# Adding x for two tiles at once with four 64x64 products at the end of an attention and spectral-mixing kernel

## The chip, the cores and the metric

The kernel runs on one core of one Trainium2 chip. The metric is the device time of one execution in microseconds (us). The engines are called PE (TensorE), DVE (VectorE), ACT (ScalarE), POOL (GpSimd) and SP (SyncE, which issues the loads and stores here).

## The reference

Two layers are computed one after the other. The first is attention with a sliding window of 128 and a linear bias per head; the second keeps the 64 lowest modes of a Fourier transform along the sequence, multiplies each mode by a complex 512x512 matrix, transforms back and adds a ReLU branch.

```
scores = scale * q @ k^T ; mask: 0 <= rel < 128 ; bias = -slope[h] * |rel|
attn = softmax(scores) ; x = attn @ v          # [8, 576, 512] after joining 8 heads of 64
X = rfft(x, axis=1)[:, :64]                    # Xr, Xi
Yr = Xr @ w_r - Xi @ w_i ; Yi = Xr @ w_i + Xi @ w_r      # 64 modes, 512x512 each
y = irfft(Y, n=576, axis=1)
u = x + y
return u + max(u @ w_ch, 0)
```

## The kernel before

The work on the attention is done in units of one pair of heads and one batch entry; the result x stays on chip in bf16 as `g.x_sb` (128 rows at a time, four such tiles per batch entry) and `g.x4` (the last 64 rows of two batch entries in one tile). `g.seq` lists the 36 tiles of x in the order in which they are finished: for an even batch entry four tiles, for the odd one behind it four, then their shared tile, so nine for two batch entries.

The weights of the modes, 134 MB, stream through a ring of three buffers per matrix (`_load_w`, line 586), and `_modes` (lines 621 and 625) multiplies one mode at a time. The first group of 128 input rows is done beside the attention, the other 384 rows, the last group, in a stage of its own. In that stage, after some of the modes, one tile of x is taken further: `_xt` transposes it and `_xw` (line 669) multiplies it by w_ch. `_xw` leaves x @ w_ch in SBUF as two bf16 parts, a rounded one and its remainder (`g.hl`, lines 673 and 674). For tiles of way "q" (line 87) x itself is added in the same PSUM tile by one more product (line 667).

When the modes are done, `_finish` runs over the 36 tiles. For each tile i PE issues, through `_pair` (two products of 64 output columns at tile positions (0, 0) and (0, 64), line 656):

- the hl pair into `mm[i]` (x @ w_ch, for way q with x in it), in `_known`;
- for way "a" the x pair into `y[i]`, also in `_known`;
- a pair of inverse transform times ZW into `mm[i]` and a pair of inverse transform times Z into `y[i]`.

`mm` and `y` have three PSUM buffers each (`fps`). For i = 0, 1 and 2 `_known` is issued before the last four modes, for the others in the loop. One turn later the tile is evacuated. Way a: ACT makes r = relu(mm) (line 783), and a turn after that DVE adds y (line 792) and SP stores the tile. Way q: ACT copies y to SBUF (line 786), DVE makes r = max(mm, x) (line 787), a turn later POOL adds the two (line 795), and another turn later SP stores. r and ys have four buffers, o has six. Before the change 18 tiles are of way a and 18 of way q.

The last four modes of all batch entries come late: `_z_late` computes them for four batch entries at once (lines 707 and 713), and `_z_take` copies one batch entry's rows to SBUF three tiles ahead of the first tile that needs them, ZW on ACT (line 723), Z on DVE (727) or ACT (725). All engines follow the order in which the program issues (`manual_schedule`).

Of the kernel before, what the change touches and what calls it, by code (L numbers as in the profile page):

```python
# [9 lines left out]
FP32 = mybir.dt.float32  # L10
# [6 lines left out]
P = 128  # L17
# [17 lines left out]
def kernel(  # L35
# [10 lines left out]
    nc = tc.nc  # L46
# [5 lines left out]
    g = Ctx()  # L52
# [30 lines left out]
    for b in range(B):  # L83
        g.seq += [(g.x_sb[:, b, st], ((b, st * P), (b, st * P + 64))) for st in range(4)]
        if b % 2:
            g.seq.append((g.x4[:, b // 2], ((b - 1, 4 * P), (b, 4 * P))))
    g.way = ["q" if 2 <= i < len(g.seq) - 5 and i % 5 in (0, 2, 3) else "a" for i in range(len(g.seq))]

    with tc.manual_schedule(engines={ET.SP, ET.PE, ET.Activation, ET.DVE, ET.Pool}):
        with ExitStack() as wctx:  # L90
# [4 lines left out]
            with ExitStack() as actx:  # L95
# [63 lines left out]
                for n in range(3, N + 2 + TAIL):  # L159
# [9 lines left out]
                    h = (len(w) + 1) // 2  # L169
# [14 lines left out]
            with ExitStack() as xctx:  # L184
                xt = xctx.enter_context(tc.tile_pool(name="xts", bufs=2))
                xps = xctx.enter_context(
                    tc.tile_pool(name="xps", bufs=2, space=bass.MemoryType.PSUM))
                eps = xctx.enter_context(
                    tc.tile_pool(name="eps", bufs=1, space=bass.MemoryType.PSUM))
                todo, done, k = list(tiles[last]), 0, 0  # L190
                xT = _xt(g, 0, xt, xps)
                while done < NM - 4:
                    m0, mg = todo.pop(0)
                    _modes(g, last, m0, mg, last=True)
                    done = m0 + mg

                    while k < len(g.seq) and k * (NM - 4) < done * len(g.seq):
                        nxt = _xt(g, k + 1, xt, xps) if k + 1 < len(g.seq) else None
                        _xw(g, k, xT, xps)
                        xT, k = nxt, k + 1  # L200
                    if 5 <= done < 9:
                        _ft(g, done - 5, xt, xps)
                    for b in range(B):
                        if m0 <= NM - 14 + b < done:
                            _z_early(g, b, eps)
# [3 lines left out]
            for i in range(3):  # L209
                _known(g, i)  # L210
# [4 lines left out]
            for m0, mg in todo:  # L215
                _modes(g, last, m0, mg, last=True)
                if NM - 4 <= m0 < NM - 1:
                    for i in range(BUSY):
                        nc.tensor.matmul(
                            idle, lhsT=g.ident_b, rhs=g.x_sb[:, i % B, 0], start=True, stop=True)  # L220
# [432 lines left out]
def _pair(nc, out, lhsT, rhs, **kw):  # L653

    for h in range(2):
        nc.tensor.matmul(  # L656
            out[64 * h : 64 * h + 64], lhsT=lhsT[h], rhs=rhs[h], tile_position=(0, 64 * h), **kw)


def _xw(g, n, xT, psum):  # L660


    nc = g.nc
    x = g.seq[n][0]
    xw = psum.tile([P, g.DM], FP32, tag="xw", name="xw")
    if g.way[n] == "q":
        nc.tensor.matmul(xw, lhsT=g.ident_b, rhs=x, start=True, stop=False)
    for dt in range(4):
        nc.tensor.matmul(xw, lhsT=xT[:, dt], rhs=g.wch[:, dt],  # L669
                         start=(dt == 0 and g.way[n] != "q"), stop=(dt == 3))  # L670
    for h in range(2):
        hi, lo = slice(64 * h, 64 * h + 64), slice(64 - 64 * h, 128 - 64 * h)
        nc.scalar.copy(g.hl[hi, n, h], xw[hi])  # L673
        nc.vector.tensor_tensor(  # L674
            out=g.hl[lo, n, h], in0=xw[hi], in1=g.hl[hi, n, h], op=ALU.subtract)


def _z_early(g, b, psum):
# [40 lines left out]
def _z_take(g, b):  # L719
    nc = g.nc  # L720
    zp, zwp = g.late
    ks = slice(32 * (b % 4), 32 * (b % 4) + 32)
    nc.scalar.copy(g.ZW[ks, b], zwp[ks])
    if b % 4 == 2:
        nc.scalar.copy(g.Z[ks, b], zp[ks])
    else:
        nc.vector.tensor_copy(g.Z[ks, b], zp[ks])


def _known(g, i):  # L730

    nc = g.nc
    x = g.seq[i][0]
    g.mm[i] = g.fps.tile([P, g.DM], FP32, tag="mm", name="mm")
    g.y[i] = g.fps.tile([P, g.DM], FP32, tag="y", name="y")
    _pair(nc, g.mm[i], [g.ident2] * 2, [g.hl[:, i, h] for h in range(2)], start=True, stop=False)
    if g.way[i] == "a":
        _pair(nc, g.y[i], [g.ident_b[:, 0:64], g.ident_b[:, 64:128]], [x] * 2,
              start=True, stop=False)


def _finish(g):
# [5 lines left out]
    with ExitStack() as fctx:  # L748
# [4 lines left out]
                 for b in range(g.B)]  # L753
        _z_late(g, 0, lps)
        _z_take(g, 0)
        o, r, y = {}, {}, {}

# [7 lines left out]
        for i in range(N + 3):  # L765
            if i < N:
                if i >= 3:
                    _known(g, i)
                ft = [g.FT[:, b % 4, s : s + 64] for b, s in g.seq[i][1]]
                _pair(nc, g.mm[i], ft, [g.ZW[:, b] for b, _ in g.seq[i][1]],  # L770
                      start=False, stop=True)
                _pair(nc, g.y[i], ft, [g.Z[:, b] for b, _ in g.seq[i][1]],
                      start=(g.way[i] == "q"), stop=True)
            if i == first[3] - 1:
                _z_late(g, 4, lps)
            for b in range(1, g.B):
                if i == first[b] - 3:
                    _z_take(g, b)
# [50 lines left out]
```

## Time and profile before

| what | value |
|---|---|
| median of 3 runs | 463.44 us (461.84 to 464.57) |
| span of the profiled execution, first to last instruction | 460.1 us |
| the profiled execution's own time | not given apart from the span; the median is 3.3 us above the span |
| PE busy | 326.6 us (71%), 5939 matmuls |
| DVE, ACT, POOL busy | 226.3 us (49%), 187.9 us (41%), 149.6 us (33%) |
| DMA | 173.92 MB, 378 GB/s in the mean |
| mean granted TensorE clock | 0.754 |

A busy time counts when any instruction of the engine ran. In lines of groups the columns are line, engine, operation, output and inputs, shapes and count, then busy time, mean duration in ns and idle time before them with what ended it. In the timeline they are start, duration, engine, line, operation and count.

### The profile page before, as it was taken

The page shows a single profiled execution, that of the slowest core. Times are in us where ns is not written, and L with a number is a line of the kernel's source. Part 1 is how long each engine was busy: PE and PEld are TensorE (multiplying, and loading weights), DVE is VectorE, ACT ScalarE, POOL GpSimd, SP SyncE. Part 2 cuts the span into 40 slices and gives each one's busy share as a digit, 9 for nine tenths or more (in the row PEclk, how much of TensorE's full clock was granted, in tenths as well). Part 3 has the DMA queues.
Part 4 walks back from the last instruction along what each step waited for, and adds up shares of the span by engine and source line. Part 5 has one row for each costly group of instructions (what it writes and reads, how often), then busy time and mean ns, then how long its engine had stood idle before and what let it go on. Part 6 is the DMA issues. An engine that isn't in the chain of part 4 may idle for free.

```text
span 460.1 us, 14005 instructions
## 1 busy us (share of the span) xinstructions
PE 326.6 (71%) x5939; PEld 229.5 (50%) x5939; DVE 226.3 (49%) x492; ACT 187.9 (41%) x345; POOL 149.6 (33%) x255
## 2 busy tenths in 40 slices
PE   2778797797868985576646655566566578877994
PEld 2557576676757864343334433333333345534552
DVE  8776588658666572333323233133331334512884
ACT  3986576576664660223212122122221123412883
POOL 7697799677676522000000000000000000000882
PEclk9985689768895796566665577566655759979999
DMA  8999999999999999999999999999999999994697
GB/s 251 309 352 326 343 335 394 389 383 381 387 386 396 388 355 362 418 426 358 422 425 423 421 425 424 422 424 425 424 421 424 424 423 401 421 425 182 234 332 258
DMA packets 68382, 173.92 MB, mean 378 GB/s; under 512 B 5600, under 2 KB 21984, under 8 KB 68320
## 3 DMA queue, kind: packets, MB, share of 16 engines
q1 hardware_dynamic: 67936, 171.99, 96.9%
q0 software_dynamic: 384, 1.05, 0.9%
q8 instruction: 46, 0.75, 0.6%
q14 instruction: 16, 0.13, 0.1%
HBM read 163.58 MB, written 9.44 MB: 376 GB/s over the span
## 4 chain that ended last, share of the span: by engine, by line
DMA 48%; PE 32%; issue 6%; ACT 5%; DVE 3%; POOL 3%; SPq 2%; ACTq 0%; POOLq 0%; DVEq 0%
DMA wi<-in_moe_w_i_dram 42%; PE sc L428 6%; PE acc L625 4%; DMA v<-in_v_dram 4%; PE acc L621 4%; PE tqk L402 4%; PE av L481 3%; PE xt L523 3%; PE xw L669 2%; PE mm L656 2%; ACT qkT L410 1%; PE tp L647 1%; PE y L656 1%; SPq L345 1%; ACT hl L673 1%
## 5 line engine op out<-in xcount | busy, mean ns | idle before, releaser
L673 ACT CAST hl<-xw 64x512 bf16<-64x512 f32 x72 | 41.8, 580 | 165.2 <-PE xw L669 137.4
L625 PEld LDWEIGHTS <-wi 128*128 128x128 bf16 x1024 | 66.1, 104 | 79.6 <-DMA wi<-in_moe_w_i_dram 72.9
L795 POOL TENSOR_TENSOR o<-r,ys 128x512 f32<-128x512 f32 x18 | 22.5, 1277 | 247.1 <-DVE r L787 245.0
L625 PE MATMUL acc<-Xlast,wi 128*128 128x16 bf16 x768 | 56.0, 193 | 53.7 <-DMA wi<-in_moe_w_i_dram 53.7
L440 ACT ACTIVATE att<-sc 128x512 bf16<-128x512 f32 (+1 forms) x128 | 72.4, 592 | 45.2 <-PE sc L428 44.5
L621 PEld LDWEIGHTS <-wr 128*128 128x128 bf16 x1024 | 70.0, 106 | 41.9 <-DMA wr<-in_moe_w_r_dram 24.5
L674 DVE TENSOR_TENSOR hl<-xw,hl 64x512 bf16<-64x512 f32 x72 | 49.6, 689 | 83.2 <-ACT hl L673 83.1
L621 PE MATMUL acc<-Xlast,wr 128*128 128x16 bf16 x768 | 62.8, 194 | 21.7 <-DMA wr<-in_moe_w_r_dram 18.0
L391 POOL CAST vb<-v 64x256 bf16<-64x256 f32 x128 | 65.3, 510 | 28.8 <-PE av L481 19.4
L443 DVE TENSOR_TENSOR att<-att,mask 128x512 bf16<-128x512 bf16 x96 | 50.7, 556 | 31.2 <-ACT att L440 30.9
L428 PE MATMUL sc<-qkT,qkT 64*64 64x256 bf16 (+1 forms) x512 | 54.2, 325 | 12.5 <-ACT att L440 5.1
L669 PE MATMUL xw<-wch,xT 128*128 128x512 bf16 x144 | 60.1, 563 | 0.0
L649 DVE COPY xT<-tp 128x512 bf16<-128x512 bf16 x36 | 15.2, 423 | 58.3 <-PE tp L647 57.9
L410 ACT COPY qkT<-tqk 128x576 bf16<-128x576 bf16 x64 | 41.1, 644 | 4.9 <-PE tqk L402 4.9
L402 PE MATMUL tqk<-ident_b,qkb 64*64 64x64 bf16 x1152 | 33.1, 213 | 13.1 <-POOL qkb L380 8.7
L428 PEld LDWEIGHTS <-qkT 64*64 64x64 bf16 x512 | 31.5, 127 | 20.3 <-issue 11.3
L402 PEld LDWEIGHTS <-qkb 64*64 64x64 bf16 x1152 | 32.4, 129 | 15.4 <-POOL qkb L380 10.4
L481 PE MATMUL av<-vb,att 64*128 64x65 bf16 (+1 forms) x1024 | 31.8, 211 | 3.5 <-issue 3.5
L481 PEld LDWEIGHTS <-att 64*128 64x128 bf16 (+1 forms) x1088 | 26.7, 109 | 9.4 <-issue 5.9
L669 PEld LDWEIGHTS <-xT 128*128 128x128 bf16 x144 | 18.7, 135 | 21.6 <-issue 19.1
L380 POOL CAST qkb<-k 128x576 bf16<-128x576 f32 x32 | 26.1, 816 | 0.3 <-PE tqk L402 0.3
L380 POOL CAST qkb<-q 128x576 bf16<-128x576 f32 x32 | 23.7, 739 | 4.8 <-PE tqk L402 1.6
(107 smaller groups left out, 440.7 us busy)
## 6 DMA issues: line engine op xcount, KB each, us to landing
wr<-in_moe_w_r_dram SPq DMA_DIRECT2D x85, 768.0 KB, 8.3
wi<-in_moe_w_i_dram SPq DMA_DIRECT2D x85, 768.0 KB, 9.7
q<-in_q_dram SPq DMA_DIRECT2D x32, 288.0 KB, 7.2
k<-in_k_dram SPq DMA_DIRECT2D x32, 288.0 KB, 7.3
v<-in_v_dram SPq DMA_DIRECT2D x64, 128.0 KB, 6.5
out_dram<-o SPq DMA_DIRECT2D x32, 256.0 KB, 2.8
vt<-in_v_dram POOLq DMA_DIRECT2D x8, 128.0 KB, 7.2
wchf<-in_moe_w_ch_dram SPq DMA_DIRECT2D x2, 512.0 KB, 7.9
```

The costliest lines, as they stand in the source:

```text
L380: g.nc.gpsimd.tensor_copy(tb, t)
L391: g.nc.gpsimd.tensor_copy(o[64 * hh : 64 * hh + 64, i], u.v[64 * i : 64 * i + 64, hh])
L402: g.nc.tensor.transpose(tp[hs, r, :], u.b[w][hs, r], g.ident_b[hs, hs], tile_position=(64 * hh, 64 * hh))
L428: nc.tensor.matmul(sc[hs, r * nq : (r + 1) * nq], lhsT=kT[hs, kt * P + r : kt * P + P : 2], rhs=qT[hs, kt * P : kt * P + nq], start=True, ...
L440: nc.scalar.activation(a[:, :cols], sc[:, :cols], AF.Exp, scale=1.0 / math.sqrt(g.D))
L443: nc.vector.tensor_tensor(out=a, in0=a, in1=g.mask[:, s], op=ALU.mult)
L481: nc.tensor.matmul(av[o, hh, col(t)], lhsT=a[hs, c0 : c0 + m], rhs=vb[hs, 0 : D + 1], start=(j == 0), stop=(j == len(terms) - 1), tile_pos ...
L621: nc.tensor.matmul(o, lhsT=wr[:, a].bitcast(BF16)[:, 1::2][:, c], rhs=X[:, a, 1:3, :, m], start=(a == 0), stop=False)
L625: nc.tensor.matmul(o, lhsT=wi[:, a].bitcast(BF16)[:, 1::2][:, c], rhs=X[:, a, 0:2, :, m], start=False, stop=(a == A - 1))
L669: nc.tensor.matmul(xw, lhsT=xT[:, dt], rhs=g.wch[:, dt], start=(dt == 0 and g.way[n] != "q"), stop=(dt == 3))
L673: nc.scalar.copy(g.hl[hi, n, h], xw[hi])
L674: nc.vector.tensor_tensor(out=g.hl[lo, n, h], in0=xw[hi], in1=g.hl[hi, n, h], op=ALU.subtract)
```

## The change

The ways are laid out in a pattern of nine: tiles 0, 1, 4 and 5 of nine are of way a, the others q, and the last three tiles are a. That makes 19 tiles of way a and 17 of way q. Tiles 0 and 1, and tiles 4 and 5, of each nine form a twin. For the second tile of a twin `_xw` exchanges the upper and lower 64 rows of x in place: a pair of products with the identity into a buffer of the `xw` tag, and a copy by ACT. In `_known` the first tile of a twin then takes two y buffers and issues four products of 64x64, one in each quadrant of the array, which add x for both tiles; the second tile issues none. In `_z_take` the Z copy of batch entries 3 and 7 moves from DVE to ACT, where those of 2 and 6 already are.

```
-    g.way = ["q" if 2 <= i < len(g.seq) - 5 and i % 5 in (0, 2, 3) else "a" for i in range(len(g.seq))]
+    g.way = ["a" if i % 9 in (0, 1, 4, 5) else "q" for i in range(len(g.seq))]
+    g.way[-3:] = ["a"] * 3
+    g.twin = {i: i + 1 for i in range(len(g.seq) - 3) if i % 9 in (0, 4)}
...
     # _xw, at its end
+    if n in g.twin.values():
+        sw = psum.tile([P, g.DM], FP32, tag="xw", name="sw")
+        _pair(nc, sw, [g.ident_b[:, 64:128], g.ident_b[:, 0:64]], [x] * 2, start=True, stop=True)
+        nc.scalar.copy(x, sw)
...
     # _z_take
-    if b % 4 == 2:
+    if b % 4 >= 2:
         nc.scalar.copy(g.Z[ks, b], zp[ks])
...
     # _known
-    x = g.seq[i][0]
     g.mm[i] = g.fps.tile([P, g.DM], FP32, tag="mm", name="mm")
-    g.y[i] = g.fps.tile([P, g.DM], FP32, tag="y", name="y")
+    if i not in g.y:
+        g.y[i] = g.fps.tile([P, g.DM], FP32, tag="y", name="y")
     _pair(nc, g.mm[i], [g.ident2] * 2, [g.hl[:, i, h] for h in range(2)], start=True, stop=False)
-    if g.way[i] == "a":
+    if i in g.twin:
+        j = g.twin[i]
+        g.y[j] = g.fps.tile([P, g.DM], FP32, tag="y", name="y")
+        for t, up in ((i, 0), (j, 64)):
+            for h in range(2):
+                ks = slice((64 * h + up) % P, (64 * h + up) % P + 64)
+                nc.tensor.matmul(
+                    g.y[t][64 * h : 64 * h + 64], lhsT=g.ident_b[ks, ks], rhs=g.seq[t][0][ks],
+                    start=True, stop=False, tile_position=(ks.start, 64 * h))
+    elif g.way[i] == "a" and i not in g.twin.values():
+        x = g.seq[i][0]
         _pair(nc, g.y[i], [g.ident_b[:, 0:64], g.ident_b[:, 64:128]], [x] * 2,
               start=True, stop=False)
```

## The prediction

> **What bounds the kernel now.** I read the page's slices first, then the end in windows, its groups by form, its waits, and last its timeline on TensorE (PE). Until about 421 us the DMA engines are the limit:
>
> ```profile
> PEclk9985689768895796566665577566655759979999
> DMA  8999999999999999999999999999999999994697
> ```
>
> One digit is 11.5 us: the DMA row is at 9 from slice 2 to slice 36, so work that other engines do beside the weight loads is free as long as it does not hold back the next load. The change adds a little there. The rest of it lies behind 421 us, in `_finish`:
>
> ```profile
> 428.00:432.00 4.00, 3.85 (x36) 2.31 (x34) 3.84 (x7) 3.81 (x8) 3.73 (x4) 1.00 0.80 301
> 436.00:440.00 4.00, 4.00 (x40) 2.18 (x38) 3.59 (x7) 3.63 (x8) 3.87 (x4) 1.00 0.96 338
> 444.00:448.00 4.00, 3.66 (x34) 2.19 (x31) 3.09 (x6) 3.93 (x8) 3.39 (x3) 1.00 0.76 291
> L656 PE MATMUL y<-x_sb,ident_b 128*64 128x512 bf16 x28 | 5.7, 382 | 0.8 <-DVE o L792 0.5 <-ACT ys L786 0.3
> DVE o L792 <- DMA out_dram<-o: 1.9, 3, 0.9
> ```
>
> The columns of a window are its length, then busy time of PE, weight load, DVE, ACT and POOL, granted clock, DMA share and GB/s. PE, DVE, ACT and POOL are all nearly full, so this stage is four balanced engines coupled by three `mm` and three `y` buffers. In the timeline a busy PE starts a pair of 64-column products every 0.215 us:
>
> ```profile
> 432.68 0.41 PE L656 MATMUL mm<-ZW,FT 128*64 128x512 bf16 x2
> 432.90 0.41 PE L656 MATMUL y<-Z,FT 128*64 128x512 bf16 x2
> 433.24 1.09 PE L707 MATMUL zwl<-wch,ZT 128*32 128x512 bf16 x16
> 434.15 0.42 PE L713 MATMUL zl<-ident_b,ZT 128*32 128x128 bf16 x16
> 434.50 0.41 PE L656 MATMUL mm<-hl,ident 128*64 128x512 bf16 x2
> ```
>
> From the first ZW product (423.85) to the last pair (453.74) PE starts 72 mm/y pairs, 33 hl pairs and 16 x pairs (three hl and two x were done before): 121 x 0.215 = 26.0 us, and 1.3 us of `_z_late`. Starts further apart than 0.215 give the waits: 428.66 to 429.23 (0.36 over), 440.17 to 440.80 (0.42), 444.52 to 444.92 (0.19), 446.86 to 447.62 (0.55), 451.57 to 452.45 (0.67), two smaller ones 0.2: 2.4 us. So PE is what sets the end, at 92%, and its waits come from buffers that ACT or DVE free late; the longest is the tail's, where DVE's o waits for a store 0.94 us (451.70).
>
> **Part 1, the x products in `_finish`.** Before: 18 tiles of way a, 16 of their x pairs on the path, 16 x 0.215 = 3.44 us. After: 8 twins and 3 single tiles; the twin (0, 1) is issued before the last modes, so 7 quads and 3 pairs stay. If the four products run at once, the quads stream 7 x 0.215. No row shows four 64x64 quadrants at once. The nearest: two 64x64 products on the diagonal do overlap (8 of 256 columns in 0.40 us, 159.76 to 160.16, where one by one at the 0.107 us that 256 columns take would be 0.85), and four of 32 columns do (16 of 512 in 0.91 us above). The ends are 0.215 and 0.43 per quad; I take 0.215, since these rows show both kinds of division overlapping. But a quad changes the tile size from 128x64 to 64x64 and back. The rows above price that: 432.90 to 433.24 is 0.34, 0.125 over a pair's 0.215; the 16 zl products stream 4 x 0.053 = 0.21 and the next pair comes 0.35 later, 0.14 over. Thus a quad costs 0.215 + 0.125 + 0.14 = 0.48, where two pairs cost 0.43. Sum: 7 x 0.48 + 3 x 0.215 = 4.0, against 3.44: **+0.55 us**. Ends: -1.3 without any price for the switch (7 x 0.215 + 3 x 0.215 = 2.15), +2.05 with quads of 0.43.
>
> The Trainium skill, TensorEngine Tiling (Array Packing), section Key Properties, says that changing the tiling mode, not just the tile, drains TensorE; by its promise in the same section that tiles operate independently alone, x would be 1.3 us cheaper, by the drain rule it is not. The trace agrees with the drain, 0.125 and 0.14 us.
>
> **Part 2, the waits.** A quad writes y of two tiles, so with three y buffers it waits until tile i-2 and i-3 are both evacuated; a single x pair needed only one free buffer. Behind that wait on PE stand the FT pairs of tile i, and behind these ACT, DVE and the stores. Twins start at i%9 = 0 and 4.
> At i%9 = 4 the two buffers are those of the ys copy of tile 2 (of the nine) and of the o add of tile 1, and DVE reaches that add late. With hl of tile 0 at time 0, by the spacings above: quad 0.34, mm0 0.70, y0 0.91, mm1 1.34, mm2 1.99, y2 2.20, hl4 3.06, quad 4 ready at 3.40. ACT starts 0.44 after a pair starts (432.90 to ys at 433.34) and takes 0.6: ys of the tile before 0.22, then ZW of `_z_take` (0.58) about 0.83, r0 1.4 to 2.0. DVE takes 0.69 and starts every 0.61: o0 2.03, then r2 (emitted ahead of o1) 2.64, o1 3.25 to 3.94. So quad 4 starts at 3.99, 0.6 late. Where `_z_take` also puts Z on ACT, which the change does for b = 3 and 7 (twins at 13 and 31), r0, o0 and o1 are 0.49 later (ZW at 427.51, Z at 428.00): 1.1 late. Sum over tiles 4, 13, 22, 31: 0.6 + 1.1 + 0.6 + 1.1 = 3.4 us.
> At i%9 = 0 (9, 18, 27) both are way q, or freed earlier, and the copy of tile i-2 ends 1.1 us after its y pair started, about when the quad is ready: 0.
> Against this all 2.4 us of old waits go: their places (y after a, q by turns) vanish, and in the tail o of tile 31 to 34 reuse buffers of tiles 25 to 28, of which 27 and 28 are now stored straight from DVE and not after POOL (1277 ns). What is late next is r on ACT. **+1.0 us**; ends -1.7 (o1 in time at all four, 0.7 of other waits) and +2.5 (all four 1.1, half of the old waits stay).
>
> **Part 3, DVE, ACT, POOL.** One q tile becomes a: POOL 17 adds, 21.7 us instead of 22.5; DVE 36 adds as before, and six Z copies become four, -1.4; ACT +1.1 (2 x 0.57). By start spacing (0.61, 0.5 to 0.6) DVE stays under 25 and ACT under 27 of some 31 us: none becomes the limit by its sum, and the place where ACT's Z is late is in part 2. Stores: 40 DMAs before and after; those of q tiles still go one turn later than those of a. Nothing.
>
> **Part 4, the exchange in `_xw`.** Eight times a pair (0.215 at full clock, 0.43 at half), two switches and an ACT copy of 0.59, in the stage where PE is busy 23.4 of 40 us and ACT 7.9. The cover is the weight ring, three modes deep, some 3.7 us each. It is thin in two places: DMA was down to 0.80 in 214 to 218 and 0.95 in 386 to 390, just where tiles 5 and 32 are exchanged. Ends 0 and +1.2 (both delays of 0.6 passed on); I take **+0.3**.
>
> **Sum.** 0.55 + 1.0 + 0.3 = 1.85 us on the profiled span of 460.1; the median of the runs, 463.44, is 3.3 above that span, which I leave as it is: 465.2, 0.4% up.
>
> **Rivals.**
> First, slower by more: the four products go two at a time. For it: no row shows four. Then PE streams 7 x 0.215 = 1.5 us more: 466.7. It decides from a quad of about 0.3 us upward. Chance 0.20.
> Second, faster: switches hide in the waits (an engine that waits anyway drains for nothing) and o1 comes in time since DVE has two Z less. Then x is 1.3 cheaper and half of the old waits go, 1.2, with the exchange free: 461.0. Against it: r2 stands ahead of o1 on DVE whatever the load. Chance 0.13.
> Third, it does not do what it says: what PE saves is waited for at the y buffers, so gain and loss cancel, 463.4. For it: four engines above 90% in the same windows. Chance 0.22.
> The forecast itself has 0.45, with an own range of 463.7 to 466.8.
>
> **Numbers.** 0.5%, about what a measurement of this kernel can tell from no change, is 2.3 us: bounds 461.1 and 465.8. Of the forecast's 0.45 a third lies above (0.15), of the first rival 0.17, and 0.03 of the third: slower 0.35. Of the second rival 0.07, and 0.01 of the third lies below: faster 0.08. Same is 0.57. The range runs from 461.6, most of the way to the second rival, to 467.6, over the first one with the upper end of part 2.
>
> **What would show it.** Right: quads whose four products start within some 0.1 us, with gaps of 0.1 to 0.15 before and after; PE idle before the quads of tiles 4, 13, 22, 31, released by DVE o; 0.5 us or more longer from the first ZW product to the last o; the stage before 421 us within 0.5 us of now. Wrong: quads of 0.4 us (first rival); no gap around them, or no wait for o (second); a loss ahead of 421 us above 1 us would break part 4.

## The result and the profile after

The change makes the kernel slower by a little: 464.56 us in the median of 22 runs against 462.78 us of the kernel before in as many; the ratio is 1.0046, with a 95% interval of 1.0025 to 1.0067. That is 2.1 us more (1.2 to 3.1). The forecast was 1.85 us, 0.4%, and the time named, 465.2 us, lies 0.6 us above the one measured. The forecast had started from 463.44 us, the median of three runs; that of 22 is 0.7 us lower. The profiled execution has a span of 463.0 us, 2.9 us above that of before.

The slices of the page, one digit for 11.6 us:

```profile
PEclk9989597978876785556575578556665569958998
DMA  8999999999999999999999999999999999992787
```

The DMA row is full up to the end of the modes as it was; the four slices behind it are the end that the change is about. The same windows as before (length, then busy time of PE, weight load, DVE, ACT, POOL, granted clock, DMA share, GB/s):

```profile
428.00:432.00 4.00, 3.53 (x30) 1.62 (x30) 2.78 (x6) 3.02 (x6) 2.51 (x2) 1.00 0.61 228
436.00:440.00 4.00, 4.00 (x58) 2.17 (x58) 3.04 (x6) 2.06 (x5) 2.58 (x3) 1.00 0.84 278
444.00:448.00 4.00, 3.76 (x32) 1.62 (x30) 3.13 (x6) 2.90 (x6) 3.07 (x3) 1.00 0.73 231
```

The same window does not hold the same work in both kernels: the change is some 1.7 us behind, and its 436 to 440 holds `_z_late`, which came at 433 before. So the stretch from y of tile 3 to the last y says more. Before it is 27.97 us, in which PE, DVE, ACT and POOL are busy for 26.8, 23.7, 22.5 and 22.5; in the change it is 29.85 us, with 28.4, 22.2, 23.5 and 21.2. DVE and POOL do less, ACT does more by the two Z copies, and PE is busy 1.7 us longer and stays at 95 to 96%. The groups by form, and of the waits of the end the one shown before (who waited for whom, us, times, longest):

```profile
L749 PE MATMUL y<-x_sb,ident_b 64*64 64x512 bf16 x28 | 4.1, 397 | 0.6 <-DVE o L808 0.5 <-ACT ys L802 0.2
L749 PEld LDWEIGHTS <-ident_b 64*64 64x64 bf16 x28 | 1.1, 103 | 4.2 <-issue 4.2
```

```profile
DVE o L808 <- DMA out_dram<-o: 0.8, 1, 0.8
```

L749 is the quad. Its weight loads stand idle for 4.2 us in front ("issue": nothing that the profile shows held them). The first load of each quad starts with its first product (428.07 for both in the quad of tile 4), while the loads of a pair start with the pair ahead of it: here the loads do not run ahead across a change of tile size. DVE's wait for a store, 1.9 us before, is down to 0.8. Two quads in the timeline of PE, of tile 4 and of tile 9 (start, duration):

```profile
427.73 0.41 PE L658 MATMUL mm<-hl,ident 128*64 128x512 bf16 x2
428.07 0.40 PE L749 MATMUL y<-x_sb,ident_b 64*64 64x512 bf16 x2
428.70 0.40 PE L749 MATMUL y<-x_sb,ident_b 64*64 64x512 bf16 x2 [0.23 <-DVE o L808]
429.03 0.41 PE L658 MATMUL mm<-ZW,FT 128*64 128x512 bf16 x2
...
432.53 0.41 PE L658 MATMUL mm<-hl,ident 128*64 128x512 bf16 x2
432.87 0.41 PE L749 MATMUL y<-x_sb,ident_b 64*64 64x512 bf16 x4
433.21 0.41 PE L658 MATMUL mm<-ZW,FT 128*64 128x512 bf16 x2
433.45 0.38 PE L658 MATMUL y<-Z,FT 128*64 128x512 bf16 x2
```

In the second quad all four products start at 432.87 and end together: they run at once. From hl to the next mm it takes 0.68 us where a pair apart would be 0.215 and two x pairs in between 0.645. So the quad does not repay what it costs in changes of tile size. In the first the half for the second tile of the twin starts 0.63 us behind the first, when DVE has finished o of tile 1 (427.96 + 0.68 = 428.64).

To compare the end of all kernels I use one stretch, from the y pair of tile 3 (all engines are under way by then) to the end of the last o, and beside it what remains from there to the end of the span, where the last stores drain. For the y pairs the start of the second product counts. Each figure is from the one profile of that kernel, so how much it varies from one execution to the next is not shown; only the last column has an interval.

| kernel | y of tile 3 to last y on PE | to the end of the last o | behind it | sum of the last two | ratio of the runs (95%) |
|---|---|---|---|---|---|
| before | 27.97 | 29.55 | 4.74 | 34.29 | |
| the change | 29.85 | 31.49 | 3.97 | 35.46 | 1.0046 (1.0025 to 1.0067) |
| pairs_for_quads | 29.17 | 30.80 | 4.11 | 34.91 | 1.0005 (0.9974 to 1.0036) |
| no_twins | 27.46 | 29.27 | 4.48 | 33.75 | 0.9982 (0.9949 to 1.0015) |
| diagonal_64 | 30.12 | 31.70 | 3.94 | 35.64 | 1.0025 (0.9997 to 1.0053) |
| z_back_to_dve | 28.65 | 30.23 | 4.32 | 34.55 | 1.0018 (0.9985 to 1.005) |
| o_first | 28.90 | 30.73 | 4.75 | 35.48 | 1.004 (1.0006 to 1.0074) |
| z_on_act | 27.97 | 29.91 | 3.94 | 33.85 | 0.9977 (0.9937 to 1.0017) |
| ways_z2 | 26.49 | 28.62 | 4.78 | 33.40 | 1.001 (0.9975 to 1.0046) |
| ways_zdve | 26.91 | 28.98 | 4.82 | 33.80 | 0.9984 (0.9943 to 1.0024) |
| ways_z2_o8 | 26.47 | 27.99 | 5.07 | 33.06 | 0.9988 (0.9962 to 1.0015) |
| before_o8 | 27.25 | 28.77 | 5.08 | 33.85 | 0.9976 (0.9951 to 1.0) |

Where the 2.9 us between the two profiled spans are: the last product of the last mode starts 0.7 later (421.46 and 422.17), of which 0.5 is there at the first transpose of x (179.48 and 179.94), ahead of every changed instruction; from there to y of tile 3 it takes 1.0 longer (4.34 and 5.38), the stretch is 1.9 longer, and 0.8 comes back behind the last o. The 1.0 us is the granted clock: in the change the zwl products start 0.43 us apart at half the clock, before 0.215. Six of the twelve profiles have such a half clock behind the last mode, runs with twins and without, so I do not count it to the change. What is left as the effect of the twins and ways is 1.2 us in the sum of the table, the low end of what the runs show; whether the rest is more than chance in the two profiles, these runs do not say.

### The profile page after: what moved, and what is told of

Read it like the earlier page. It is cut to its first block, busy times and chain, and to the rows that moved or that the text cites. A ratio compares the mean times of both kernels' runs of the same rounds, so it can differ in the third digit from the quotient of the medians.

```text
span 463.0 us, 14019 instructions
## 1 busy us (share of the span) xinstructions
PE 331.5 (72%) x5928; PEld 227.4 (49%) x5956; DVE 224.1 (48%) x490; ACT 193.9 (42%) x355; POOL 149.7 (32%) x254
## 4 chain that ended last, share of the span: by engine, by line
DMA 46%; PE 34%; issue 6%; ACT 5%; DVE 4%; POOL 3%; SPq 1%; ACTq 0%; POOLq 0%; DVEq 0%
DMA wi<-in_moe_w_i_dram 41%; PE sc L430 6%; DMA k<-in_k_dram 5%; PE acc L627 4%; PE acc L623 4%; PE av L483 3%; PE tqk L404 3%; PE xt L525 3%; PE mm L658 3%; PE xw L671 2%; PE y L658 1%; PE tp L649 1%; POOL qkb L382 1%; ACT qkT L412 1%; ACT hl L675 1%
## 5 line engine op out<-in xcount | busy, mean ns | idle before, releaser
L811 POOL TENSOR_TENSOR o<-r,ys 128x512 f32<-128x512 f32 x17 | 21.2, 1274 | 251.7 <-DVE r L803 246.6
L393 POOL CAST vb<-v 64x256 bf16<-64x256 f32 x128 | 67.3, 525 | 28.3 <-PE av L483 18.8
L671 PE MATMUL xw<-wch,xT 128*128 128x512 bf16 x119 | 52.9, 569 | 4.9 <-issue 2.4
```

What stands on the lines that cost most here:

```text
L393: g.nc.gpsimd.tensor_copy(o[64 * hh : 64 * hh + 64, i], u.v[64 * i : 64 * i + 64, hh])
L671: nc.tensor.matmul(xw, lhsT=xT[:, dt], rhs=g.wch[:, dt], start=(dt == 0 and g.way[n] != "q"), stop=(dt == 3))
```

## The experiments

My theory: PE is what the end waits for; a quad pays two changes of tile size, which eats what it saves, and since it needs the y buffers of two tiles at once PE waits for buffers. Rivals: the changes of tile size hide in waits; the pattern of ways and the Z copies cost everything; the exchange in `_xw` costs (part 4 of the next section).

**The quads as pairs (pairs_for_quads).** Everything else of the change is kept.

```
-            for h in range(2):
-                ks = slice((64 * h + up) % P, (64 * h + up) % P + 64)
-                nc.tensor.matmul(g.y[t][64 * h : 64 * h + 64], lhsT=g.ident_b[ks, ks], rhs=g.seq[t][0][ks], ...)
+            _pair(nc, g.y[t], [g.ident_b[:, up : up + 64], g.ident_b[:, 64 - up : 128 - up]],
+                  [g.seq[t][0]] * 2, start=True, stop=False)
```

> The change with each quad replaced by two ordinary pairs at the same place in the program: both y buffers are still taken at the first tile of a twin and the exchange in _xw stays; only the change of tile size goes. My theory (the size change costs PE 0.27 us a quad on the path, and streaming four at once saves 0.215): 7 x (0.43 - 0.48) = -0.4 us against the change; the waits for the second y buffer at tiles 4, 22 and 31 stay, some 0.4 us each. Rival 1 (the size change hides in waits, the streaming counts): 7 x 0.215 = +1.5 us against the change.

Measured: 0.69 us less than the change up to the last o, 0.55 in the sum. The rival's +1.5 is out: four products at once bring nothing here over two pairs. That they lose rests on one profile of each, since the runs (0.9974 to 1.0036, against 1.0025 to 1.0067) do not separate the two. The wait for the second buffer is still there, 0.77 us between the two pairs of tile 22:

```profile
447.06 0.41 PE L658 MATMUL mm<-hl,ident 128*64 128x512 bf16 x2
447.27 0.41 PE L658 MATMUL y<-x_sb,ident_b 128*64 128x512 bf16 x2
448.04 0.41 PE L658 MATMUL y<-x_sb,ident_b 128*64 128x512 bf16 x2 [0.36 <-DVE o L805]
448.25 0.41 PE L658 MATMUL mm<-ZW,FT 128*64 128x512 bf16 x2
```

There is also no gap around the pairs: 447.06, 447.27 and 448.04, 448.25 lie 0.21 apart, where the quad has 0.34 on both sides.

**No twins (no_twins).** `g.twin = {}`: the pattern of ways and the Z copies alone.

> The change with an empty list of twins: the new pattern of ways and the Z copies on ACT stay, every tile of way a adds its x by its own pair, no exchange in _xw. My theory: on PE 17 x pairs on the path, 3.65 us instead of 4.0, and the waits for a second y buffer (0.41, 0.43 and 0.37 us in the profile of the change) go: -1.6 us against the change, so +0.5 us against the kernel before; the waits of hl 8, 12, 25 and 29 for r on ACT stay. Rival 2 (the twins are innocent, the pattern of ways and the Z copies cost everything): equal to the change, +2 us against the kernel before.

Measured: 2.22 us less than the change up to the last o, 1.71 in the sum, and 0.28 less than the kernel before, where I had expected 0.5 more. The runs say so too: their interval ends at 1.0015, that of the change begins at 1.0025. The rival (the twins are innocent) is out: the loss goes with them, and the pattern of ways with the Z copies costs nothing. The exchange in `_xw` is left out here as well; pairs_for_quads, which keeps it, and part 4 below show no cost of it.

**A change of tile size alone (diagonal_64).** In the kernel before each x pair becomes two 64x64 products on the diagonal.

```
-        _pair(nc, g.y[i], [g.ident_b[:, 0:64], g.ident_b[:, 64:128]], [x] * 2, start=True, stop=False)
+        for h in range(2):
+            ks = slice(64 * h, 64 * h + 64)
+            nc.tensor.matmul(g.y[i][ks], lhsT=g.ident_b[ks, ks], rhs=x[ks],
+                             start=True, stop=False, tile_position=(64 * h, 64 * h))
```

> The kernel before with each x pair replaced by two 64x64 products on the diagonal of the array: the same streaming time of 0.215 us, the same buffers and waits, but a change of tile size before and after each of the 16 x additions on the path. My theory: 16 x (0.125 + 0.14) = +4.2 us against the kernel before, less what falls into its 2.4 us of waits on PE, so +3 to +4.2. Rival 1 (a size change hides beside the other engines): under 1 us.

The price is as expected, the effect is not:

```profile
447.10 0.38 PE L656 MATMUL mm<-hl,ident 128*64 128x512 bf16 x2
447.41 0.40 PE L740 MATMUL y<-x_sb,ident_b 64*64 64x512 bf16 x2
447.74 0.41 PE L656 MATMUL mm<-ZW,FT 128*64 128x512 bf16 x2
447.98 0.38 PE L656 MATMUL y<-Z,FT 128*64 128x512 bf16 x2
```

0.31 and 0.33 between starts instead of 0.215, and 0.24 once behind: 0.24 per addition, 3.8 us for 16. But up to the last y on PE it took only 2.15 us more, because waits of before shrank to make room. So a change of tile size is real PE time, of which rather over half reached the last y and 1.35 us, a good third, the end of the span. My 3 to 4.2 missed. The rival's "under 1" missed by the profile; by the runs (0.25%, interval -0.03 to 0.53%) it cannot be excluded, nor told whether the kernel is slower at all.

**Z back to DVE (z_back_to_dve).** `if b % 4 == 2` in the change.

> The change with the Z copies of batch entries 3 and 7 back on DVE. My theory: the waits of hl 12 and 29 for r (0.23 us each) and of y 12 and 30 for o (0.27 us each) that the profile of the change has behind ZW and Z on ACT go or halve: -0.5 to -1 us against the change. Rival 3 (DVE is what is late, and the move to ACT helped): +0.5 us or more against the change.

Measured: 1.26 us less than the change up to the last o, 0.91 in the sum. The waits at tile 12 that the change has are these (gaps of 0.42 ahead of hl and 0.51 ahead of y):

```profile
434.74 0.38 PE L658 MATMUL y<-Z,FT 128*64 128x512 bf16 x2
435.16 0.41 PE L658 MATMUL mm<-hl,ident 128*64 128x512 bf16 x2
435.38 0.41 PE L658 MATMUL mm<-ZW,FT 128*64 128x512 bf16 x2
435.89 0.41 PE L658 MATMUL y<-Z,FT 128*64 128x512 bf16 x2
```

With Z on DVE no starts from hl of tile 10 to `_z_late` lie further than 0.23 apart (tile 10 and 11: 432.02, 432.23, 432.45, 432.66, 432.88). So in the presence of twins the two Z copies on ACT cost about 1 us, by one profile of each; the runs (1.0018 against 1.0046) do not separate the two kernels.

**Z on ACT without the rest (z_on_act).** The opposite: `if b % 4 >= 2` in the kernel before.

> The kernel before with the Z copies of batch entries 3 and 7 on ACT and nothing else of the change. My theory (ZW and Z in a row on ACT delay r, whose mm buffer the next hl pair needs): the stretch from y of tile 3 to the end of the last o grows from 29.55 us by 0.5 to 1. Rival (ACT has room, the move only hurts together with the twins): within 0.2 us of 29.55.

Measured: +0.36 us up to the last o and -0.44 in the sum; the runs say 0.9977 (0.9937 to 1.0017). Less than I expected, more than the rival said, and no loss at the end. The wait of the theory, hl for r, shows at tile 12 alone: 0.46 us between starts (432.61 and 433.07) instead of 0.215. More is lost at x of tile 29, from 0.76 to 1.24 us between starts (447.46 and 448.70), which waits for the copy ys on ACT and so for a y buffer, while the wait of the tail goes. What the Z copies cost depends on what else is late.

**o ahead of r (o_first).** In the change, the block of o of tile i-2 stands ahead of that of r and ys of tile i-1.

> The change with the order of emission inside a turn of _finish altered: o of tile i-2 (DVE and POOL) ahead of r and ys of tile i-1. It takes r2 out of the way of o1 on DVE. My theory (the second y buffer is late because r stands ahead of o1): the splits inside the quads of tiles 4, 22 and 31 (0.63, 0.64 and 0.58 us between the two halves in the profile of the change) shrink to nothing or a third, from y of tile 3 to the end of the last o 31.5 us becomes some 30.5; 1 us less than the change. Rival (the buffer is late for another reason, or r that comes later stops PE at mm instead): 31.5 us as before, the waits move to the hl pairs.

The quad of tile 4 now runs at once:

```profile
427.27 0.41 PE L658 MATMUL mm<-hl,ident 128*64 128x512 bf16 x2
427.61 0.45 PE L749 MATMUL y<-x_sb,ident_b 64*64 64x512 bf16 x4
427.99 0.41 PE L658 MATMUL mm<-ZW,FT 128*64 128x512 bf16 x2
...
430.17 0.38 PE L658 MATMUL y<-Z,FT 128*64 128x512 bf16 x2
430.79 0.41 PE L658 MATMUL mm<-hl,ident 128*64 128x512 bf16 x2 [0.24 <-ACT r L807]
431.00 0.41 PE L658 MATMUL mm<-ZW,FT 128*64 128x512 bf16 x2
431.26 0.41 PE L658 MATMUL y<-Z,FT 128*64 128x512 bf16 x2
432.11 0.41 PE L658 MATMUL mm<-hl,ident 128*64 128x512 bf16 x2 [0.44 <-DVE r L811]
```

So the order on DVE was the reason for the split of this quad: that part of the theory is shown. The gain is not what I said: the hl pair of tile 9 now waits for an r on DVE that was pushed back (432.11, 0.85 after the pair ahead of it), and the longest wait is new, at the y pair of tile 25 (447.32, 1.03 after the pair ahead) for an o on DVE, which by the profile had itself waited for Z on ACT. Up to the last o 0.76 us are won, behind it 0.78 are lost, and the runs are as slow as those of the change. The rival was right in that waits moved to the hl pairs, though not to them alone.

**The ways alone (ways_z2, ways_zdve).** No twins; Z copies as before, or all on DVE.

> Only the new pattern of ways: no twins, no exchange, Z copies as in the kernel before. In the run without twins the stretch from y of tile 3 to the end of the last o was 29.27 us, with waits at hl 12, y 12, hl 29 and y 30 of 0.23 and 0.27 us each behind ZW and Z on ACT. My theory: these go, 28.3 to 28.6 us, 1 us below the kernel before, 0.2% of the whole. Rival (the pattern of nine needs the relief of DVE): 29.3 or more.

> The new pattern of ways without twins and exchange, and all Z copies on DVE. My theory: also the waits of hl 8 and hl 25 (0.18 us each) behind ZW and Z of batch entries 2 and 6 go, but DVE, with 44 copies and adds at 0.61 us, comes near 27 us: 28.0 to 28.8 us from y of tile 3 to the last o. Rival (DVE becomes what is late): over 29.3.

Measured: 28.62 and 28.98 us up to the last o, each slightly above the range expected, 0.93 and 0.57 under the kernel before; in the sum 0.89 and 0.49. The runs cannot tell either from the kernel before.

**Eight o buffers (ways_z2_o8, before_o8).** `tag="o", bufs=8`. This was meant as a version that beats both.

> The run ways_z2 (pattern of nine, no twins, no exchange, Z copies as before) with eight o buffers instead of six. In ways_z2 the last o waits 0.54 us for a store and POOL 1.5 us for two. My theory: 0.4 to 0.8 us less from y of tile 3 to the end of the last o, 27.8 to 28.2 us, so 1.4 to 1.7 us under the kernel before. Rival (the stores themselves limit the tail): 28.6 as in ways_z2, and what is saved there comes back behind the last o.

> The kernel before with eight o buffers instead of six. My theory: the waits of its tail (o of DVE 0.94 us for a store, and through it PE 0.67 us at the x pair of tile 34) go: from y of tile 3 to the end of the last o 28.7 us instead of 29.55. Rival (the stores limit): 29.5, or a longer time behind the last o.

Measured: 27.99 and 28.77 us up to the last o, as expected, and PE's longest wait in the tail of before is gone; behind the last o 0.3 us come back, as the rivals said in part. In the sum 1.23 and 0.44 us under the kernel before. The ratios of the runs are 0.9988 (0.9962 to 1.0015) and 0.9976 (0.9951 to 1.0): neither is clear of no change. A version that is shown to beat the kernel before I have not found; the profiles put ways_z2_o8 first, by 0.3%, which is the size of its interval.

## Why the prediction was right

**The time.** In the stretch at the end the change costs 1.9 us, where parts 1 and 2 say 1.55. Behind the last o 0.8 us comes back, which the sum did not have, and of the 1.7 us that the profile adds ahead of the stretch 0.5 came before any changed instruction and 1.0 with the half clock, which runs without twins have too. So that the time came within 0.6 us is in part luck. (463.44 + 1.85 is 465.3; the prediction writes 465.2.)

**Part 1, +0.55 us.** Right in its terms. In the trace a quad goes in 0.31 after the last product of the pair ahead of it, its four products start within 0.01 us, and 0.33 later the next pair starts: 0.46 us over a sequence without it, 0.48 with the 0.02 that the y pair loses. That is the 0.48 that the change from the 32-column products had given. 7 x 0.48 + 3 x 0.215 = 4.0 us. The first rival (two at a time) is out: no quad whose buffers were free was split. The rule of the Trainium skill that was weighed, that changing the tiling mode drains TensorE (TensorEngine Tiling (Array Packing), section Key Properties), agrees with this trace at 0.12 to 0.14 us for each change. In diagonal_64 part of this price fell into waits that were there anyway.

**Part 2, +1.0 us.** Near in its sum, wrong in its places. What PE waits between y of tile 3 and the last y is the stretch less the work: before 27.97 - 112 pairs x 0.215 - 1.4 for `_z_late` = 2.5; in the change 29.85 - 99 x 0.215 - 7 x 0.48 - 1.4 = 3.8. So 1.3 us more, where 3.4 - 2.4 = 1.0 was said. Of the four quads at i%9 = 4, those of tiles 4 and 22 wait 0.6 us for the o add of tile 1 of the nine, as worked out from DVE's order. That of tile 31 waits 0.6 too, not 1.1, and not for that add: its second half is released by ACT, at the end of the copy ys of tile 30.

```profile
452.44 0.41 PE L658 MATMUL y<-Z,FT 128*64 128x512 bf16 x2
453.00 0.40 PE L749 MATMUL y<-x_sb,ident_b 64*64 64x512 bf16 x2
453.58 0.40 PE L749 MATMUL y<-x_sb,ident_b 64*64 64x512 bf16 x2 [0.18 <-ACT ys L802]
```

The copy runs from 452.94 to 453.53, late because y of tile 30 (452.44) had waited for o of tile 27. With the Z copies on DVE (z_back_to_dve) the same quad waits for DVE's o, 0.64 us between its halves. The quad of tile 13 waits nothing: `_z_late` stands ahead of it on PE (436.22 to 437.48), which I had left out, and the copies ys that free its buffers are done by 436.97. So the quads give 1.8 instead of 3.4. The missing term is the other ring: `mm` has three buffers as well, and with ZW and Z in a row on ACT the r that frees one is late:

```profile
446.66 0.58 ACT L729 CAST ZW<-zwl 32x512 bf16<-32x512 f32 x1
447.15 0.57 ACT L731 CAST Z<-zl 32x512 bf16<-32x512 f32 x1
447.75 0.60 ACT L799 ACTIVATE r<-mm 128x512 f32<-128x512 f32 x1
...
447.77 0.38 PE L658 MATMUL y<-Z,FT 128*64 128x512 bf16 x2
448.39 0.41 PE L658 MATMUL mm<-hl,ident 128*64 128x512 bf16 x2 [0.24 <-ACT r L799]
```

hl of tile 26 starts when r of tile 23 ends (448.35), 0.62 after the pair ahead of it. Such waits at hl 8, 12, 26 and 30 (the expectations call the last two 25 and 29) make 1.2 us, and those of y 12 and 30 for o another 0.6, on tiles where I had put nothing. Single waits add to 3.7, the stretch gives 3.8. That the sum is near is luck: 1.6 us too much at the quads stands against 2.0 that it lacked elsewhere. (Its upper end, +2.5, is not what its terms give: 4 x 1.1 less half of 2.4 is 3.2.) The tail went as said: there the x pairs of tiles 33 to 35 no longer wait.

**Part 3, nothing.** Right by its sums: no engine became the limit. The cost of the Z copies I had put at the quads alone; z_back_to_dve shows it, about 1 us, most of it at hl and y of tiles 12 and 30. The waits of hl 8 and 26, 0.8 us together, stand behind Z copies that were on ACT before the change too, and stay in that run.

**Part 4, +0.3 us.** Not seen. From the first transpose of x to the last product of the last mode the four profiles with the exchange take 242.2, 243.4, 241.7 and 243.0 us, the eight without it 241.4 to 244.0. They are no longer with it, but a cost of 0.3 would not show in such a spread, and whether the weight ring covers the exchange at the two places that I called thin stays open. The stage ended 0.7 later, over the 0.5 that was named as a sign; 0.5 of this was there before any changed instruction ran.

**The rivals.** The third (gains and losses cancel) had the wrong picture of the gain: there was none on PE to cancel. The second is out, since PE waited for o as r2 stood ahead of it, which o_first shows.

## What to carry to other kernels

Price a packed product with its neighbours: if the products ahead of and behind it have another tile size, two changes of 0.12 to 0.14 us belong to it, and it must save more than that. Where a fusion writes two tiles at once, count the buffers it takes at once and find in the emission order who frees the older one; here that was an add queued behind a max on DVE (at one quad a copy on ACT), which no total of busy time shows. And with four engines near full and rings of three, do not add up waits tile by tile as if they stayed in place: a wait removed in one ring (o_first) or a price added (diagonal_64) came back or was absorbed by half elsewhere.

## What the hardware showed that I had not expected

Four 64x64 products in the four quadrants, each in the same rows as one of the others and in the same columns as another, start within 0.01 us and take the time of one (432.87). And behind the last mode the granted clock is at a half for some 3.4 us in six of twelve profiles (PE 0.43 us per pair instead of 0.215), in others not at all; that alone is 1 us between two profiles, half of what the change does. Why it falls there or not, no run here tells.
